# Attention of batch b+1 emitted between the MLP chunks of batch b, with 128-token tiles and a softmax with a constant bias

## The chip, the cores and the metric

The kernel runs on one core of one Trainium2 chip. Times are device microseconds of that core for one execution. Of the kernel before, three runs are known: 1060.54, 1063.5 and 1299.54 us, median 1063.5. A profile of one execution is there as well.

## The reference

Eight batches, twelve heads, 448 tokens, head size 64. Queries and keys are normalised over the head size, attention is a plain softmax over all 448 keys, the heads are joined to 768 columns, and a LayerNorm and an MLP of width 3072 with a residual follow.

```python
def rmsnorm(x, g):
    rms = np.sqrt(np.mean(x * x, axis=-1, keepdims=True) + 1e-06)
    return x / rms * g
q_n, k_n = (rmsnorm(q, g_q), rmsnorm(k, g_k))
scores = scale * np.matmul(q_n, k_n.transpose(0, 1, 3, 2))     # scale = 1/8
scores = scores - np.max(scores, axis=-1, keepdims=True)
attn = np.exp(scores)
attn = attn / (np.sum(attn, axis=-1, keepdims=True) + 1e-09)
x = np.matmul(attn, v)                          # heads joined: (8, 448, 768)
xn = (x - mu) / np.sqrt(var + 1e-06) * g_ln     # mu, var over 768
out = x + np.maximum(xn @ w_ch1, 0.0) @ w_ch2   # 768 -> 3072 -> 768
```

Inputs and output are float32; the matmuls are done in float16 with float32 accumulation, the keys as a high and a low float16 part.

## The kernel before, in words

Tokens lie in four tiles of 112 partitions; token 4p+s is row p of tile s.

*Preparation* (`emit_prep`, L143 to L188) takes a quarter of a batch, three heads: loads of q and k on the SP queue, squares on ACT (L153, L154), sums and an inverse root on DVE (`_rsqrt`, L20 to L29: a start value by exponent bits, one exponential on ACT, three Newton steps), the scaled query (L166), the key times both gains and its inverse root (L170, L174), its high part (L179) and low part (L180). Column 63 of the low part is overwritten by 1 (L181). Values come by casting DMAs on the POOL queue (L185) into v16, whose column 64 is 1.

*One head* (`emit_heads`, L190 to L242): PE transposes query (L198), key high (L201) and key low (L204), four tiles each; DVE and ACT copy them to SBUF (L208 to L210). Four small matmuls against the first 64 keys (L213) give an estimate of each query's maximum (L216), which POOL writes, negated, into column 63 of the query (L217). The query is transposed once more (L221, L223), now with that column. So the score matmul, 128 rows deep (query twice; key high over key low), subtracts the estimate by itself. L227 makes 112 keys by 448 queries, L228 the exponential on ACT, in float16. Sixteen matmuls of 65 columns (L234) multiply by the values and, in column 64, sum the denominator; L239 and L240 divide and write x_sb.

*One MLP* (`emit_mlp`, L95 to L141): LayerNorm on DVE (L104, L105, `_rsqrt`, L111, L113 with the gain), 24 transposes (L118) and copies (L121) to xnT, 768 by 448. Up: 24 groups of six matmuls of 448 columns (L126), each followed by a Relu on ACT (L128). Down: six groups of 24 matmuls (L132) that give 128 output columns by 448 tokens, that is channel-major; each is copied to SBUF (L135), transposed back in float32 four times (L138) and added to x_sb (L139). One store per batch (L141).

*Order.* The program emits all attention, one quarter prepared ahead of the heads, and then the eight MLPs (L244 to L259). The framework then lists the instructions of each engine: an instruction that is ready by the framework's own estimate is taken by the place at which it was emitted, and a tile must wait for a free buffer. x_sb has three buffers (L86), so attention of a fourth batch waits for the first MLP; from there on attention and MLP mix. On the chip each engine keeps the listed order. Weights come by casting DMAs on the POOL queue (L76 to L81); nothing holds them back, so they start at once. PSUM: psQ and psKhl one buffer each, scores two, psO one, MLP three (L88 to L91).

Of the kernel before, what the change touches and what calls it, by code (L numbers as in the profile page):

```python
# [13 lines left out]
AX = mybir.AxisListType  # L15
ts = bass.ts
LN2 = 0.6931471805599453


def _rsqrt(nc, eng, out, a, t0, t1, iters=3):  # L20
    eng.tensor_copy(out=t0, in_=a.bitcast(INT32))
    eng.tensor_scalar(out=t0, in0=t0, scalar1=2.0 ** -23, scalar2=-127.0,
                      op0=ALU.mult, op1=ALU.add)
    nc.scalar.activation(out, t0, AFT.Exp, scale=-0.5 * LN2)
    for _ in range(iters):
        eng.tensor_tensor(out=t1, in0=out, in1=out, op=ALU.mult)
        eng.tensor_tensor(out=t1, in0=t1, in1=a, op=ALU.mult)
        eng.tensor_scalar(out=t1, in0=t1, scalar1=-0.5, scalar2=1.5, op0=ALU.mult, op1=ALU.add)
        eng.tensor_tensor(out=out, in0=out, in1=t1, op=ALU.mult)  # L29


@with_exitstack
def kernel(
# [12 lines left out]
    nc = tc.nc  # L46
    B, H, S, Dh = q.shape
    Dm = H * Dh
    P1 = 112
    NS = S // P1  # L50
    NQ = 4
    HH = H // NQ
    GH = HH * NS
    FF = moe_w_ch1.shape[1]
    NDC = Dm // 128
    NNC = FF // 128

    const = ctx.enter_context(tc.tile_pool(name="const", bufs=1))
    id16 = const.tile([128, 128], FP16)
    make_identity(nc, id16)  # L60
    id32 = const.tile([128, 128], FP32)
    make_identity(nc, id32)
    gq_bc = const.tile([P1, Dh], FP32)
    gk_bc = const.tile([P1, Dh], FP32)
    nc.sync.dma_start(gq_bc, g_q.unsqueeze(0).broadcast_to([P1, Dh]))
    nc.sync.dma_start(gk_bc, g_k.unsqueeze(0).broadcast_to([P1, Dh]))
    gprod_bc = const.tile([P1, Dh], FP32)
    nc.vector.tensor_tensor(out=gprod_bc, in0=gq_bc, in1=gk_bc, op=ALU.mult)
    gln_bc = const.tile([P1, Dm], FP32)
    nc.sync.dma_start(gln_bc, moe_g_ln.unsqueeze(0).broadcast_to([P1, Dm]))  # L70

    w_pool = ctx.enter_context(tc.tile_pool(name="w_pool", bufs=1))
    w1_sb = w_pool.tile([128, NDC, NNC, 128], FP16)
    w2_sb = w_pool.tile([128, NNC, Dm], FP16)

    def emit_w_load():  # L76
        for dc in range(NDC):
            nc.gpsimd.dma_start(
                out=w1_sb[:, dc],
                in_=moe_w_ch1[ts(dc, 128), :].rearrange("p (nc c) -> p nc c", c=128))  # L80
        nc.gpsimd.dma_start(out=w2_sb, in_=moe_w_ch2.rearrange("(nc p) d -> p nc d", p=128))  # L81

    a_io = ctx.enter_context(tc.tile_pool(name="a_io", bufs=2))
    a_tmp = ctx.enter_context(tc.tile_pool(name="a_tmp", bufs=1))
    a_hd = ctx.enter_context(tc.tile_pool(name="a_hd", bufs=2))
    x_pool = ctx.enter_context(tc.tile_pool(name="x_pool", bufs=3))  # L86
    m_tmp = ctx.enter_context(tc.tile_pool(name="m_tmp", bufs=1))
    ps_tr = ctx.enter_context(tc.tile_pool(name="ps_tr", bufs=1, space=bass.MemoryType.PSUM))  # L88
    ps_s = ctx.enter_context(tc.tile_pool(name="ps_s", bufs=2, space=bass.MemoryType.PSUM))
    ps_o = ctx.enter_context(tc.tile_pool(name="ps_o", bufs=1, space=bass.MemoryType.PSUM))  # L90
    ps_m = ctx.enter_context(tc.tile_pool(name="ps_m", bufs=3, space=bass.MemoryType.PSUM))  # L91

    x_tiles = []

    def emit_mlp(b):  # L95
        x_sb = x_tiles[b]
        xn16 = m_tmp.tile([P1, NS, Dm], FP16, tag="xn16")
        stat = m_tmp.tile([P1, NS, 16], FP32, tag="stat")
        lt0 = m_tmp.tile([P1, NS], FP32, tag="lt0")
        lt1 = m_tmp.tile([P1, NS], FP32, tag="lt1")  # L100
        rstd = m_tmp.tile([P1, NS], FP32, tag="rstd")
        for s1 in range(NS):
            for sg in range(2):
                nc.vector.bn_stats(out=stat[:, s1, ts(sg, 6)], in_=x_sb[:, s1, ts(sg, Dm // 2)])  # L104
            nc.vector.bn_aggr(out=stat[:, s1, 12:14], in_=stat[:, s1, 0:12])  # L105
        nc.vector.tensor_scalar(out=stat[:, :, 14], in0=stat[:, :, 13], scalar1=1.0, scalar2=1e-6,
                                op0=ALU.mult, op1=ALU.add)
        _rsqrt(nc, nc.vector, rstd, stat[:, :, 14], lt0, lt1)
        for s1 in range(NS):
            t32 = m_tmp.tile([P1, Dm], FP32, tag="t32", bufs=1)  # L110
            nc.vector.tensor_scalar(out=t32, in0=x_sb[:, s1], scalar1=stat[:, s1, 12:13],  # L111
                                    scalar2=rstd[:, s1:s1 + 1], op0=ALU.subtract, op1=ALU.mult)
            nc.vector.tensor_tensor(out=xn16[:, s1], in0=t32, in1=gln_bc, op=ALU.mult)  # L113
        xnT = m_tmp.tile([128, NDC, S], FP16, tag="xnT")
        for dc in range(NDC):
            pst = ps_m.tile([128, 512], FP16, tag="mlpacc")
            for s1 in range(NS):
                nc.tensor.matmul(pst[:, ts(s1, P1)], xn16[:, s1, ts(dc, 128)],  # L118
                                 id16[0:P1, 0:P1], is_transpose=True,
                                 start=(s1 == 0), stop=(s1 == NS - 1))  # L120
            nc.vector.tensor_copy(out=xnT[:, dc], in_=pst[:, 0:S])  # L121
        hT16 = m_tmp.tile([128, NNC, S], FP16, tag="hT16")
        for ncc in range(NNC):
            psH = ps_m.tile([128, S], FP32, tag="mlpacc")
            for dc in range(NDC):
                nc.tensor.matmul(psH, w1_sb[:, dc, ncc], xnT[:, dc],  # L126
                                 start=(dc == 0), stop=(dc == NDC - 1))
            nc.scalar.activation(out=hT16[:, ncc], in_=psH, func=AFT.Relu)  # L128
        for jc in range(NDC):
            psC = ps_m.tile([128, S], FP32, tag="mlpacc")  # L130
            for ncc in range(NNC):
                nc.tensor.matmul(psC, w2_sb[:, ncc, ts(jc, 128)], hT16[:, ncc],  # L132
                                 start=(ncc == 0), stop=(ncc == NNC - 1))
            chj = m_tmp.tile([128, S], FP32, tag="chj", bufs=1)
            nc.vector.tensor_copy(out=chj, in_=psC)  # L135
            for s1 in range(NS):
                psr = ps_m.tile([P1, 128], FP32, tag="mlpacc")
                nc.tensor.matmul(psr, chj[:, ts(s1, P1)], id32, is_transpose=True)  # L138
                nc.vector.tensor_tensor(out=x_sb[:, s1, ts(jc, 128)], in0=psr,  # L139
                                        in1=x_sb[:, s1, ts(jc, 128)], op=ALU.add)  # L140
        nc.sync.dma_start(out[b].rearrange("(p s1) d -> p s1 d", p=P1), x_sb)  # L141

    def emit_prep(b, qtr, v16, x_sb):  # L143
        hs = qtr * HH
        q_sb = a_io.tile([P1, GH, Dh], FP32, tag="q_sb")
        k_sb = a_io.tile([P1, GH, Dh], FP32, tag="k_sb")
        nc.sync.dma_start(q_sb.rearrange("p (h s1) d -> p h (s1 d)", h=HH),
                          q[b, hs:hs + HH].rearrange("h (p s1) d -> p h (s1 d)", p=P1))
        nc.sync.dma_start(k_sb.rearrange("p (h s1) d -> p h (s1 d)", h=HH),
                          k[b, hs:hs + HH].rearrange("h (p s1) d -> p h (s1 d)", p=P1))  # L150
        sq_q = a_tmp.tile([P1, GH, Dh], FP32, tag="sq", bufs=2)
        sq_k = a_tmp.tile([P1, GH, Dh], FP32, tag="sq", bufs=2)
        nc.scalar.activation(sq_q, q_sb, AFT.Square)  # L153
        nc.scalar.activation(sq_k, k_sb, AFT.Square)  # L154
        ssq = a_hd.tile([P1, 2, GH], FP32, tag="ssq")
        nc.vector.tensor_reduce(out=ssq[:, 0], in_=sq_q, axis=AX.X, op=ALU.add)
        nc.vector.tensor_reduce(out=ssq[:, 1], in_=sq_k, axis=AX.X, op=ALU.add)
        msq = a_hd.tile([P1, 2, GH], FP32, tag="msq")
        nc.vector.tensor_scalar(out=msq, in0=ssq, scalar1=1.0 / Dh, scalar2=1e-6,
                                op0=ALU.mult, op1=ALU.add)  # L160
        rrms = a_hd.tile([P1, 2, GH], FP32, tag="rrms")
        rt0 = a_hd.tile([P1, 2, GH], FP32, tag="rt0")
        rt1 = a_hd.tile([P1, 2, GH], FP32, tag="rt1")
        _rsqrt(nc, nc.vector, rrms, msq, rt0, rt1)
        qn16 = a_io.tile([P1, GH, Dh], FP16, tag="qn16")
        nc.vector.tensor_tensor(  # L166
            out=qn16, in0=q_sb,
# [122 lines left out]
```

## Time and profile before

| | |
|---|---|
| median of three runs | 1063.5 us (1060.54 to 1299.54) |
| span of the profiled execution | 1055.9 us |
| its own time | the span and a few us around it; the two lower runs lie 4.6 and 7.6 us above the span |
| mean granted TensorE clock | 0.909 |
| HBM | 52.31 MB read, 11.01 MB written |

In the profile PE is TensorE's matmuls, PEld its weight loads, DVE the vector engine, ACT the scalar engine, POOL GpSimd, SP the engine that issues most DMAs. A row of the groups reads: line, engine, operation, output and inputs, shapes, count, then busy microseconds in total and mean nanoseconds of one, then the idle time of that engine just before them and what ended it. A row of the windows reads: start and end in the span, its length, busy microseconds of the engine with the number of instructions that started, the granted clock as a share of full speed, the share of time that the DMA engines were busy, and GB/s. A row of the chain of waits in order of time reads: start, length, and the piece of work that the end was waiting for. Matmuls are pipelined, so a matmul's mean duration is longer than the distance from one to the next; the distance is had from a run of them in the chain.

### The profile page before, as it was taken

Reading aid. Unit: us, or ns where it says so; the run is one execution under the profiler, and the core shown is the slowest. Engines: PE = TensorE matmul, PEld = TensorE weight load, DVE = VectorE, ACT = ScalarE, POOL = GpSimd, SP = SyncE. Lnnn points to the kernel's source line nnn. Section 1 sums busy time; section 2 is a strip of 40 time slices with the busy share of each in tenths; the row PEclk is TensorE's granted clock in tenths of the full one; section 3 lists DMA queues with packets and bytes.
Section 4 is the critical chain, followed back from the end, with each engine's and each line's share of the span. In section 5 each row is a group of like instructions: output and inputs, shape, how many; then the busy total and the mean of one; then the engine's idle time right before and its main releaser. Section 6 shows DMA issues by size and latency. Waiting matters only on the chain.

```text
span 1055.9 us, 16343 instructions
## 1 busy us (share of the span) xinstructions
PE 908.8 (86%) x6528; PEld 552.9 (52%) x6528; DVE 625.2 (59%) x1849; ACT 400.3 (38%) x777; POOL 68.1 (6%) x183
## 2 busy tenths in 40 slices
PE   0368888888899899889998999789998998898986
PEld 0246565666554466446653566346644664444542
DVE  5457777776786378927884678647873743402111
ACT  1235544444442066404760377106730661130310
POOL 2010100100100000100010002000000000000000
PEclk9999565555589999999999999899999999999999
DMA  9891511501420101501150114110100000100101
GB/s 189 173 207 41 65 28 41 66 27 40 57 50 1 43 25 42 78 1 54 41 79 14 53 41 53 40 53 27 28 1 25 29 2 1 53 1 1 53 1 53
DMA packets 71484, 49.42 MB, mean 47 GB/s; under 512 B 45056, under 2 KB 69632, under 8 KB 70512
## 3 DMA queue, kind: packets, MB, share of 16 engines
q0 software_dynamic: 47472, 14.94, 12.9%
q1 hardware_dynamic: 23936, 33.44, 10.4%
q8 instruction: 51, 0.84, 0.3%
q14 instruction: 25, 0.20, 0.1%
HBM read 52.31 MB, written 11.01 MB: 60 GB/s over the span
## 4 chain that ended last, share of the span: by engine, by line
PE 76%; DVE 15%; DMA 4%; issue 2%; POOL 2%; ACT 1%; SPq 0%; POOLq 0%; DVEq 0%; ACTq 0%
PE psC L132 20%; PE psH L126 19%; PE psS L227 10%; PE psO L234 9%; PE psA L213 3%; PE psQ L221 3%; PE psQ L198 3%; DVE chj L135 3%; DMA q_sb<-in_q_dram 3%; PE psr L138 3%; PE psKhl L201 2%; PE psKhl L204 2%; DVE x_sb L139 2%; DVE xn L113 1%; DVE maxs L216 1%
## 5 line engine op out<-in xcount | busy, mean ns | idle before, releaser
L126 PE MATMUL psH<-xnT,w_sb 128*128 128x448 f16 x1152 | 268.4, 354 | 0.0
L228 ACT ACTIVATE E<-psS 112x448 f16<-112x448 f32 x384 | 193.9, 542 | 143.0 <-PE psS L227 137.2
L128 ACT ACTIVATE hT<-psH 128x448 f16<-128x448 f32 x192 | 103.9, 542 | 364.3 <-PE psH L126 364.0
L132 PE MATMUL psC<-hT,w_sb 128*128 128x448 f16 x1152 | 233.1, 359 | 0.0
L132 PEld LDWEIGHTS <-w_sb 128*128 128x128 f16 x1152 | 115.5, 101 | 103.3 <-issue 7.1
L234 PEld LDWEIGHTS <-E 112*112 112x112 f16 x1536 | 148.0, 156 | 39.6 <-issue 14.4
L135 DVE COPY chj<-psC 128x448 f32<-128x448 f32 x48 | 29.9, 624 | 229.4 <-PE psC L132 229.4
L227 PE MATMUL psS<-q16d,khl 128*112 128x448 f16 x384 | 148.4, 435 | 17.1 <-DVE q16d L223 13.5
L234 PE MATMUL psO<-v,E 112*112 112x65 f16 x1536 | 149.7, 234 | 0.7
L126 PEld LDWEIGHTS <-w_sb 128*128 128x128 f16 x1152 | 104.7, 100 | 77.8 <-issue 0.2
L138 PE MATMUL psr<-id,chj 128*112 128x128 f32 x192 | 41.7, 299 | 51.2 <-DVE chj L135 36.3
L227 PEld LDWEIGHTS <-khl 128*112 128x112 f16 x384 | 54.3, 150 | 33.2 <-issue 12.4
L217 POOL TENSOR_SCALAR qn<-maxs 112x4 f16<-112x4 f32 x96 | 26.6, 277 | 640.4 <-DVE maxs L216 582.6
L221 PE MATMUL psQ<-id,qn 112*64 112x112 f16 x384 | 42.7, 244 | 28.3 <-POOL qn L217 27.6
L138 PEld LDWEIGHTS psr<-id,chj 128*112 128x112 f32 x192 | 20.6, 133 | 84.1 <-DVE chj L135 57.4
L216 DVE TENSOR_REDUCE maxs<-psA 112x4 f32<-112x256 f32 x96 | 40.4, 421 | 38.4 <-PE psA L213 36.3
L198 PE MATMUL psQ<-id,qn 112*64 112x112 f16 x384 | 44.1, 248 | 20.2 <-DVE qn L166 20.2
L198 PEld LDWEIGHTS <-qn 112*64 112x64 f16 x384 | 27.2, 126 | 63.1 <-issue 42.9
L139 DVE TENSOR_TENSOR x_sb<-psr,x_sb 112x128 f32<-112x128 f32 x192 | 47.3, 286 | 19.3 <-PE psr L138 18.2
L213 PE MATMUL psA<-khl,q16d 64*112 64x64 f16 x384 | 44.4, 238 | 16.1 <-DVE khl L209 16.1
L210 ACT COPY khl<-psKhl 64x448 f16<-64x448 f16 x96 | 50.2, 523 | 17.6 <-DVE khl L209 15.1
L221 PEld LDWEIGHTS <-qn 112*64 112x64 f16 x384 | 26.7, 124 | 49.5 <-POOL qn L217 46.0
(55 smaller groups left out, 898.4 us busy)
## 6 DMA issues: line engine op xcount, KB each, us to landing
q_sb<-in_q_dram SPq DMA_DIRECT2D x32, 336.0 KB, 3.2
k_sb<-in_k_dram SPq DMA_DIRECT2D x32, 336.0 KB, 3.2
out_dram<-x_sb SPq DMA_DIRECT2D x8, 1344.0 KB, 6.2
v<-in_v_dram POOLq DMA_DIRECT2D x32, 168.0 KB, 5.8
w_sb<-in_moe_w_ch_dram POOLq DMA_DIRECT2D x6, 768.0 KB, 14.0
w_sb<-in_moe_w_ch_dram POOLq DMA_DIRECT2D x1, 4608.0 KB, 33.0
gln_bc<-in_moe_g_ln_dram SPq DMA_DIRECT2D x1, 336.0 KB, 5.7
gq_bc<-in_g_q_dram SPq DMA_DIRECT2D x1, 28.0 KB, 3.1
```

Of the source, the lines that this page charges most:

```text
L126: nc.tensor.matmul(psH, w1_sb[:, dc, ncc], xnT[:, dc], start=(dc == 0), stop=(dc == NDC - 1))
L128: nc.scalar.activation(out=hT16[:, ncc], in_=psH, func=AFT.Relu)
L132: nc.tensor.matmul(psC, w2_sb[:, ncc, ts(jc, 128)], hT16[:, ncc], start=(ncc == 0), stop=(ncc == NNC - 1))
L135: nc.vector.tensor_copy(out=chj, in_=psC)
L138: nc.tensor.matmul(psr, chj[:, ts(s1, P1)], id32, is_transpose=True)
L139: nc.vector.tensor_tensor(out=x_sb[:, s1, ts(jc, 128)], in0=psr, in1=x_sb[:, s1, ts(jc, 128)], op=ALU.add)
L198: nc.tensor.matmul(psQ[:, ts(s1, P1)], qn16[:, g0 + s1], id16[0:P1, 0:P1], is_transpose=True, start=(s1 == 0), stop=(s1 == NS - 1))
L213: nc.tensor.matmul(psA[:, ic, 0:64], q16d[0:64, ts(ic, P1)], khl[0:64, 0:64], start=True, stop=True)
L221: nc.tensor.matmul(psQ2[:, ts(s1, P1)], qn16[:, g0 + s1], id16[0:P1, 0:P1], is_transpose=True, start=(s1 == 0), stop=(s1 == NS - 1))
L227: nc.tensor.matmul(psS[:, 0:S], khl[:, ts(jc, P1)], q16d, start=True, stop=True)
L228: nc.scalar.activation(out=E16[:, jc], in_=psS[:, 0:S], func=AFT.Exp, scale=1.0 / 8.0)
L234: nc.tensor.matmul(psO[:, ic, 0:65], E16[:, jc, ts(ic, P1)], v16[:, jc, h, 0:65], start=first, stop=(ic == NS - 1 and jc == NS - 1))
```

## The change

The whole program is rewritten around the same computation. What is added, moved and removed:

- **Order.** `attention` is a generator over 49 steps, one per pair of heads and one to drain: step p has scores of pair p and values of pair p-1, and the transposes of pair p+1. `run` drives it: until step 7 there is attention alone, with loads of W1 in 12 chunks and of W2 in four between; then for each batch b the 48 or 56 chunks of the MLP of b are emitted, and after each the attention goes on so that the attention of b+1 is done at 0.78 of the chunks. Then come LayerNorm and transposes of b+1. The MLP of the last batch has no attention beside it.
- **Tiles.** A head's first 384 tokens are three full tiles of 128; the 64 left of two heads share a tile (`load_unit`: a unit is four heads, 14 groups of 128 rows, nine DMAs on SP for q, k and v in float32). The 64 left tokens of two batches share a tile in the MLP, so even batches have 384 tokens and odd ones 512.
- **Preparation** of a unit is as before without the columns of ones; the query is written twice side by side, key high and low side by side, so one transpose of 128 columns does for both. v is cast on POOL from the float32 load.
- **Softmax.** No estimate of the maximum; the exponential has the constant bias -4. The seven exponentials of a pair have 128 keys by 448 queries.
- **Check.** The reciprocals of all denominators are kept; `flag` tests before the last MLP that all lie in 1/3e7 to 0.5. At the end the flag is read, and `_general`, a loop over the batches that computes all outputs again with row maxima, runs behind a branch if one does not.
- **MLP.** The LayerNorm gain is multiplied into W1 as it is loaded (float32 load on SP, six POOL instructions a chunk). Up is as before with 384 or 512 columns. Down has 128 tokens of hT as weights and 384 columns of W2 moving, so its result is token-major and is added to x at once; the float32 transposes and the copy are gone. Stores are per token tile.
- **PSUM.** One buffer for transposes, two for scores, one each for oA and oB (values of a pair), three for the MLP.

```diff
+    def load_unit(self, u):
...
+        t = self.p_in.tile([128, 3, UG, D], FP32, tag="qkv")
+        for n, src in enumerate((self.q, self.k, self.v)):
+            nc.sync.dma_start(
+                t[:, n, 0:UH * 3].rearrange("p (h j) d -> p h (j d)", j=3),
+                src[b, hs:hs + UH, 0:384].rearrange("h (p j) d -> p h (j d)", j=3))
+            left = src[b, hs:hs + UH, 384:448].rearrange("(g e) p d -> e p g d", e=2)
+            for e in range(2):
+                nc.sync.dma_start(t[64 * e:64 * e + 64, n, UH * 3:UG], left[e])
...
+    def prep_unit(self, u):
...
+        nc.vector.tensor_tensor(out=khl[:, :, 1], in0=t[:, 1], in1=khl[:, :, 0], op=ALU.subtract)
+        nc.vector.tensor_tensor(out=qn[:, :, 0], in0=t[:, 0],
+                                in1=rr[:, 0].unsqueeze(2).broadcast_to([128, UG, D]), op=ALU.mult)
+        nc.vector.tensor_copy(out=qn[:, :, 1], in_=qn[:, :, 0])
+        v16, vl = self.v16[u % 3], self.vl[u % 3]
+        nc.gpsimd.tensor_copy(out=v16[:, :, :, 0:D],
+                              in_=t[:, 2, 0:UH * 3].rearrange("p (h j) d -> p h j d", j=3))
...
+    def trans_k(self, p):
...
+        ps = self.ps_tr.tile([128, 1024], FP16, tag="tr")
...
+        for i, g in enumerate(gs):
+            nc.tensor.matmul(ps[:, ts(i, 128)], khl[:, g], sh.id16, is_transpose=True,
+                             start=(i == 0), stop=(i == 6))
+        flat = kT.rearrange("p g d -> p (g d)")
+        nc.vector.tensor_copy(out=flat[:, 0:64], in_=ps[:, 0:64])
+        nc.vector.tensor_copy(out=flat[:, 128:960], in_=ps[:, 64:896])
...
+    def scores(self, p, i):
...
+        if i < 6:
+            h = i // 3
+            nc.tensor.matmul(ps[:, 0:S], kT[:, 192 + 128 * i:320 + 128 * i],
+                             qT[:, h * S:(h + 1) * S], start=True, stop=True)
+        else:
+            nc.tensor.matmul(ps[:, 0:S], kT[:, 0:128], qT[:, 0:S], start=True, stop=False)
+            nc.tensor.matmul(ps[:, 0:384], kT[:, 64:192], qT[:, 512:896], start=False, stop=False)
+            nc.tensor.matmul(ps[:, 384:448], kT[:, 64:192], qT[:, 448:512], start=False, stop=True)
+        nc.scalar.activation(out=c["E"][:, i], in_=ps[:, 0:S], func=AFT.Exp, scale=1.0 / 8.0,
+                             bias=EXP_BIAS)
...
+    def values(self, p, i):
...
+        for t in range(3):
+            nc.tensor.matmul(oA[:, t, cs], E[:, i, m0 + 128 * t:m0 + 128 * t + 128], rhs,
+                             start=(i == 0 and t == 0), stop=(i == 6 and t == 2))
+        nc.tensor.matmul(oB[:, cs], E[:, i, l0:l0 + 64], rhs, start=(i == 0), stop=(i == 6))
+        if i == 6:
+            self.evac_o(p)
...
+    def load_w1(self, c0, c1):
...
+        st = self.p_st.tile([128, NDC, 256], FP32, tag="st", name="st")
+        nc.sync.dma_start(st[:, :, 0:c1 - c0],
+                          self.w1[:, c0:c1].rearrange("(dc p) f -> p dc f", p=128))
+        for dc in range(NDC):
+            nc.gpsimd.tensor_scalar(out=sh.w1[:, dc, c0:c1], in0=st[:, dc, 0:c1 - c0],
+                                    scalar1=sh.gln[:, dc:dc + 1], scalar2=None, op0=ALU.mult)
...
+        def down(t, g, s):
...
+            for f in range(6 * s, 6 * s + 6):
+                nc.tensor.matmul(ps[:, 0:384], hT[:, f, ts(t, 128)], sh.w2[:, f, ts(g, 384)],
+                                 start=(f == 0), stop=(f == NFF - 1))
+            if s == 3:
+                x = tiles[t]
+                nc.vector.tensor_tensor(out=x[:, ts(g, 384)], in0=ps[:, 0:384],
+                                        in1=x[:, ts(g, 384)], op=ALU.add)
+                if g == 1:
+                    self.store(b, t, x)
...
+    def run(self):
...
+        upto(1)
+        wcols = list(range(0, FF, 256))
+        for i, c in enumerate(wcols):
+            self.load_w1(c, c + 256)
+            upto(1 + 5 * (i + 1) / len(wcols))
+        for n0 in range(0, NFF, 6):
+            self.load_w2(n0, n0 + 6)
+        upto(7)
+        xn, n = self.ln(0)
+        for t in range(n):
+            self.ln_trans(xn, n, t)
+        frac = 0.78
+        for b in range(B):
+            chunks = list(self.mlp_chunks(b))
...
+            for i, (cost, emit) in enumerate(chunks):
+                emit()
+                done += cost
+                f = done / total
+                if b + 1 < B:
+                    upto(min(goal, start + (goal - start) * f / frac))
+                    if xn is None and self.pos >= goal:
+                        xn, n = self.ln(b + 1)
...
+            if b + 2 == B:
+                upto(1e8)
+                self.flag()
...
+    val = nc.values_load(sh.flag[0:1, 0:1], min_val=0, max_val=1)
+    with tc.If(val > 0):
+        _general(tc, sh, q, k, v, g_q, g_k, out)
```

`trans_q` is `trans_k` for the query with one copy of 896 columns; `evac_o` takes two reciprocals and two products on DVE; `ln` has no gain. All lines of the functions of the kernel before are removed, `_rsqrt` stays.

More of the change, by code (lines that the diff above doesn't have):

```diff
@@ L66 @@
[L66 to L167, printed above, removed]
-            in1=rrms[:, 0].unsqueeze(2).broadcast_to([P1, GH, Dh]), op=ALU.mult)
-        kg = a_tmp.tile([P1, GH, Dh], FP32, tag="kg")
-        nc.vector.tensor_tensor(out=kg, in0=k_sb,
-                                in1=gprod_bc.unsqueeze(1).broadcast_to([P1, GH, Dh]),
-                                op=ALU.mult)
-        kn32 = a_tmp.tile([P1, GH, Dh], FP32, tag="kn32")
-        nc.vector.tensor_tensor(
-            out=kn32, in0=kg,
-            in1=rrms[:, 1].unsqueeze(2).broadcast_to([P1, GH, Dh]), op=ALU.mult)
-        knh = a_io.tile([P1, GH, Dh], FP16, tag="knh")
-        knl = a_io.tile([P1, GH, Dh], FP16, tag="knl")
-        nc.vector.tensor_copy(out=knh, in_=kn32)
-        nc.vector.tensor_tensor(out=knl, in0=kn32, in1=knh, op=ALU.subtract)
-        nc.gpsimd.memset(knl[:, :, 63], 1.0)
-        if qtr == 0:
-            nc.gpsimd.memset(v16[:, :, :, 64], 1.0)
-            for s1 in range(NS):
-                nc.gpsimd.dma_start(
-                    out=v16[:, s1, :, 0:Dh],
-                    in_=v[b].rearrange("h (p s1) d -> p s1 h d", p=P1)[:, s1])
-        return dict(hs=hs, qn16=qn16, knh=knh, knl=knl, v16=v16, x_sb=x_sb)
@@ L244 @@
[L244 to L259 removed]
+    sh = _Shared()
@@ new lines @@
+    nc.vector.tensor_tensor(out=sh.gprod, in0=gg[:, 0], in1=gg[:, 1], op=ALU.mult)
+    sh.gln = const.tile([128, NDC], FP32, name="gln")
+    nc.scalar.dma_start(sh.gln, moe_g_ln.rearrange("(c p) -> p c", p=128))
+    sh.flag = const.tile([1, 1], INT32, name="flag")
+    sh.w1 = const.tile([128, NDC, FF], FP16, name="w1")
+    sh.w2 = const.tile([128, NFF, DM], FP16, name="w2")
+    with ExitStack() as fctx:
+        _Fast(fctx, tc, sh, q, k, v, moe_w_ch1, moe_w_ch2, out).run()
+    val = nc.values_load(sh.flag[0:1, 0:1], min_val=0, max_val=1)
```

481 lines of the change are left out of this document (396 added, 85 removed).

## The prediction

> **What bounds the kernel now.** I read the page first, then the busy time by windows, then the chain of waits in order of time, and last the groups of instructions for prices.
>
> ```profile
> span 1055.9 us, 16343 instructions
> PE 908.8 (86%) x6528; PEld 552.9 (52%) x6528; DVE 625.2 (59%) x1849; ACT 400.3 (38%) x777; POOL 68.1 (6%) x183
> ...
> PEclk9999565555589999999999999899999999999999
> ...
> PE 76%; DVE 15%; DMA 4%; issue 2%; POOL 2%; ACT 1%; SPq 0%; POOLq 0%; DVEq 0%; ACTq 0%
> ```
>
> TensorE is busy for 86% of the span and carries 76% of the chain, so its program order sets the time. But its time is not all work at full speed: the granted clock drops to 0.5 in slices 5 to 10. The windows (all PE, then the score matmuls of L227 alone) say in which stage:
>
> ```profile
> 105.00:210.00 105.00, 88.17 (x652) 0.57 0.33 51
> 372.00:445.00 73.00, 69.37 (x627) 1.00 0.27 44
> ```
> ```profile
> 150.00:200.00 50.00, 16.86 (x32) 0.53 0.12 34
> 372.00:445.00 73.00, 14.79 (x48) 1.00 0.27 44
> ```
>
> Up to 299 us there is only attention (three batches, as x_sb has three buffers), and it runs at a clock of 0.57: a score matmul lasts 16.86/32 = 527 ns there and 14.79/48 = 308 ns once MLP matmuls stand between. The chain in order of time gives the pitch of each piece:
>
> ```profile
> 3.66 10.39 DMA k_sb<-in_k_dram
> ...
> 20.13 17.26 DMA q_sb<-in_q_dram
> ...
> 45.00 0.91 PE psS L227 x2
> ...
> 107.09 0.91 PE psS L227 x2
> 113.19 0.93 PE psS L227 x2
> ...
> 365.64 1.81 DVE xnT L121 x6
> ...
> 444.88 6.25 PE psC L132 x24
> 452.86 4.59 PE psC L132 x24
> ...
> 478.47 1.81 DVE xnT L121 x6
> ...
> 914.42 1.67 PE pst L118 x24
> 916.08 27.34 PE psH L126 x144
> 943.42 4.55 PE psC L132 x24
> 949.71 4.59 PE psC L132 x24
> ...
> 1041.87 4.59 PE psC L132 x24
> ```
>
> The reader sees four stages. Attention alone takes 113.19 - 107.09 = 6.1 us a head. Then one batch of attention and one of MLP take 478.47 - 365.64 = 112.8 us; in it the W2 groups start 6.3 us apart (949.71 - 943.42) with 4.55 us of matmuls, and the 1.7 us between are copy, transpose and add. The last two MLPs run alone, and the end lies 1055.9 - 1046.5 = 9.4 us behind the last W2 matmul.
>
> **The change, part by part.** Its first effect is order: MLP chunks of batch b are emitted between attention steps of batch b+1, so attention alone lasts one batch instead of three and the MLPs that run alone shrink from three (one before, two after) to one. The second is less work on PE. Prices, warm:
>
> ```profile
> 372.84 0.96 PE psO L234 x16
> ```
> ```profile
> L138 PE MATMUL psr<-id,chj 128*112 128x128 f32 x192 | 41.7, 299 | 51.2 <-DVE chj L135 36.3 <-DVE x_sb L139 15.0
> L139 DVE TENSOR_TENSOR x_sb<-psr,x_sb 112x128 f32<-112x128 f32 x192 | 47.3, 286 | 19.3 <-PE psr L138 18.2
> L240 DVE TENSOR_TENSOR x_sb<-psO,recip 112x256 f32<-112x256 f32 x96 | 40.2, 419 | 1.0
> L156 DVE TENSOR_REDUCE ssq<-sq_q 112x12 f32<-112x768 f32 x32 | 30.2, 943 | 16.1 <-ACT sq_q L153 16.1
> L170 DVE TENSOR_TENSOR kg<-k_sb,gprod_bc 112x768 f32<-112x768 f32 x32 | 30.4, 950 | 7.0 <-DMA k_sb<-in_k_dram 6.8
> L179 DVE CAST knh<-kn 112x768 f16<-112x768 f32 x32 | 17.8, 555 | 0.3
> L208 DVE COPY q16d<-psQ 64x448 f16<-64x448 f16 x96 | 36.6, 381 | 24.5 <-PE psQ L198 23.8
> L29 DVE TENSOR_TENSOR rrms<-rrms,rt 112x24 f32<-112x24 f32 x96 | 16.3, 171 | 0.7
> L104 DVE BATCH_NORM_STATS2 stat<-x_sb 112x6 f32<-112x384 f32 x64 | 33.9, 540 | 0.1
> L111 DVE TENSOR_SCALAR t<-x_sb,stat,rstd 112x768 f32<-112x768 f32 x32 | 21.7, 678 | 0.9
> L228 ACT ACTIVATE E<-psS 112x448 f16<-112x448 f32 x384 | 193.9, 542 | 143.0 <-PE psS L227 137.2 <-PE psO L234 2.6
> L153 ACT ACTIVATE sq_q<-q_sb 112x768 f32<-112x768 f32 x32 | 26.9, 841 | 49.1 <-DMA q_sb<-in_q_dram 47.3 <-DVE ssq L156 1.4
> L183 POOL MEMSET v<- 112x48 f16 x8 | 2.5, 310 | 26.9 <-PE psO L234 26.9
> L217 POOL TENSOR_SCALAR qn<-maxs 112x4 f16<-112x4 f32 x96 | 26.6, 277 | 640.4 <-DVE maxs L216 582.6 <-DVE rt L27 25.4 <-DVE recip L239 18.1
> ```
>
> *MLP matmuls.* psH runs at 27.34/144 = 190 ns, 0.424 ns a column. Up: 163 ns for 384 columns (even batches), 217 for 512 (odd). Down is now token-major, 48 matmuls of 384 columns per token tile. An even batch takes 288 x 0.163 = 47.0, an odd one 144 x 0.217 + 192 x 0.163 = 62.5 us. The pair costs what it costs now (4 x 27.3): W2 token-major saves no streaming; it removes the copies of L135, the fp32 transposes of L138 (299 ns) and the 1.7 us behind each of 48 W2 groups, at most 82 us; its one add of 384 columns per group lies beside the next group, as ps_m has three slots. LayerNorm transposes: 1.67/24 = 70 ns for 112 columns, so 76 for 128; 18 or 24 a batch, 1.4 or 1.8 us. All MLPs: 4 x 48.4 + 4 x 64.3 = 451 us.
>
> *Attention matmuls per pair of heads.* Transposes fall from 32 (query twice) to 14 of full width: 14 x 76 = 1.06 us. The eight estimate matmuls (psA) go, and with them the chain max, POOL, second query transpose. Scores keep 3584 columns: 1.52. Values: 28 instead of 32 at 0.96/16 = 60 ns: 1.68. Sum 4.26 us a pair, against 6.1 for two heads now (32 x 70 + 8 x 60 + 1.52 + 32 x 60 ns).
>
> The Trainium skill (TensorE: Matmul & The Clock Gate, Back-to-back issue gap) gives about 81 ns per matmul for a stream of weight loads and matmuls at 128 columns. By it the 42 small matmuls cost 0.66 us more a pair, some 27 us more in the sum; the 70 ns row of the same kind of stream disagrees, so I go by the row.
>
> *Start.* The first unit is nine DMAs on SP with W1 chunks behind them, W2 on POOL at once. Its landing is bounded by the two rows above, 14 us and 37 us; with about 10 us of preparation and 3 of transposes and copies the first scores come between 27 and 50 us; I take 34 (DMA is contended from the start, as now). Then seven steps of attention alone, still at the low clock: between 7.6 us a pair (DVE, below) and 9.4 (two heads at 6.1 us, with the columns 7456 instead of 9760). PE alone, at 527/308 times 4.26, is 7.3; I take 8. MLP 0 starts at 34 + 56 = 90 us (bounds 80 and 116).
>
> *Interleave.* Left are 41 pairs, 175 us, and 451 us of MLP, of which the last MLP (64) runs alone: 562 us in the interleave. How dense can PE be? Now, between 365.64 and 444.88 it fits 12 heads (37.0), 27.3 of psH, 1.7 of transposes and about 5 of psC, 71 of 79 us, 0.90, with the long chain per head in it. That chain goes, and values run one pair behind scores, so waits are shorter: 0.94, bounds 0.90 and 1. 562/0.94 = 598 us.
>
> *Other engines, costed at nothing.* DVE: from L139 and L240 an element costs 1.04 ns behind 153 fixed; L208 gives 0.51 for f16 from PSUM. Per pair: copies 64, 832, 896 columns 1.37, two reciprocals 0.36, two products 0.84: 2.6 us. Per unit of two pairs: two reductions 2.2, four products of 896 elements 4.3, casts 1.0, fifteen small ones 2.6: 10.1. So 7.6 a pair, and with LayerNorm and adds 61 us a batch, beside 80 of PE. ACT: seven exponentials 3.8 a pair, 24 Relu 13, squares 6: 42 us a batch. Both hide behind PE as long as no in-order wait puts them on its path (price: the second case below). POOL's copies of v are off the path as units are prepared two pairs ahead. SP's waits are in order too: a W1 load waiting for its staging slot, or a store waiting for its add, holds the q, k, v loads queued behind; these run two units ahead (about 27 us each). The oA and oB banks have one buffer each: values of the next pair wait for 1.2 us of DVE, and MLP chunks stand in that gap.
>
> *End.* The last add and store, then the flag is read and the branch skipped.
>
> ```profile
> out_dram<-x_sb SPq DMA_DIRECT2D x8, 1344.0 KB, 6.2
> ```
>
> The last store is a seventh of these 1344 KB. No row shows a branch; I bound it by 0 and two such landings, 12 us. Against the 9.4 us of now I take 9 behind the last matmul, the smaller store paying for most of the branch (bounds 5 and 15).
>
> Sum: 90 + 598 + 64 + 9 = 761 us of span. Around the span lie 1060.54 - 1055.9 = 4.6 to 1063.5 - 1055.9 = 7.6 us for the lowest and the median run (the profile tells nothing of the highest, 1299.54); with 5, **766 us**. The best bounds give 80 + 562 + 64 + 5 + 5 = 716, the worst 116 + 624 + 64 + 15 + 8 = 827.
>
> **The rivals.**
> *DVE paces.* At 61 of 80 us it is the next engine, its long preparation instructions stand in front of the PSUM copies, and ps_tr, oA and oB have one buffer. If the 2.6 us of each pair fall on PE's path, 41 x 2.6 = 107 us more: 873. For: "DVE 15%" of the chain now. Against: MLP chunks are independent and fill, and the window 372 to 445 shows PE at 69 of 73 us.
> *W1 comes late.* Each chunk is load, six POOL scalings, slot free. POOL's price for 256 elements is not shown: between 0.28 us (L217, four elements) and 256 x 310/48 ns = 1.65 (L183), nearer the lower end as most of such a short instruction is fixed; 72 of them take 20 to 119 us. At the upper end the last chunk stands at about 140 us, 50 late; attention of batch 1 fills some of it until its two x buffers are full: 40 us more, 806. Against: the chunks are used in order, two up steps each, so only the last must be that late.
> *The clock stays low*, the case on the other side. The place is the interleave: at 105 to 210 us PE was busy for 84% and had 0.57. If MLP beside attention did not raise it, 662 us become 662 x 527/308 = 1133: 1237 us. It decides from 63% of the interleave on (766 + 0.63 x 471 = 1063). Against: every window with MLP matmuls has 0.95 to 1.00, and their share now grows. The Trainium skill (same page, The HAM clock gate) lets activity release the throttle and idling of about 3.4 us bring it back; this trace shows 0.57 on a busy PE, so it does not agree.
> *The general path runs*, a second computation of everything. By the reference's formula the denominators of these inputs lie between 14.6 and 1442.5, allowed are 2 to 3e7. So it is skipped.
>
> **How the numbers follow.** Forecast 0.72, DVE paces 0.11, W1 late 0.13, clock low 0.03, general path 0.01. The range takes the forecast's bounds, the lowest end drawn in because all its terms would have to be best at once, and W1 late: 726 to 830. Left out are the DVE case, the low clock and the general path, 0.15. Faster by over 2% (about what a measurement of this kernel tells from no change) 0.96, within 2% 0.01, slower 0.03.
>
> **What would show it.** Right: clock above 0.9 from about a tenth of the span on; psC at 163 ns with no DVE copy between groups; the first up matmul near 90 us; PE idle under 8% until the attention ends; seven exponentials a pair on ACT. Wrong: PE waiting on DVE copies of qT and kT or on oA for more than 60 us in total; up matmuls waiting on POOL; any instruction of the general path in the trace; clock near 0.5 past 150 us.

## The result, and the profile after

| | before | after |
|---|---|---|
| median | 1062.26 us | 796.23 us (795.01 to 798.35) |
| profiled execution | span 1055.9 | 795.19, span 793.4 |
| mean granted clock | 0.909 | 0.97 |
| first up matmul of the MLP | 297.3 us | 131.4 us |

The ratio is 0.7505, with a 95% interval of 0.748 to 0.753; it leaves out one slow execution of the kernel before (1299.54 us), which the median of 1062.26 includes. The prediction was 766 us, 726 to 830. The measured time lies in that range, 30 us above the forecast, and the 30 us have one place, as the page shows at a glance:

```profile
span 793.4 us, 12901 instructions
PE 697.7 (88%) x5114; PEld 419.7 (53%) x5114; DVE 455.2 (57%) x1229; ACT 322.0 (41%) x609; POOL 119.8 (15%) x154
PE   0276438999999989999999999998999999999996
...
POOL 2579992000000000010000000010000000000000
PEclk9997777999999999999999999999999999999999
DMA  8993642523021130233022130233020110001011
```

From the seventh of forty slices on PE is dense; in the fourth to sixth it is at 0.6, 0.4 and 0.3, and there POOL is full. The windows (busy of PE, PEld, DVE, ACT, POOL, then clock, DMA share, GB/s) put numbers to it:

```profile
30.00:60.00 30.00, 20.25 (x154) 12.91 (x152) 18.41 (x45) 13.70 (x26) 22.45 (x25) 1.00 1.06 259
60.00:130.00 70.00, 36.72 (x321) 23.03 (x321) 49.71 (x137) 26.90 (x51) 63.20 (x63) 0.73 0.47 143
140.00:634.00 494.00, 479.48 (x3555) 288.25 (x3553) 319.59 (x846) 226.81 (x430) 27.07 (x51) 0.99 0.22 64
```

From 140 to 634 us PE is busy 97% at a clock of 0.99: attention and MLP mixed, as forecast. From 60 to 130 us it is busy half the time, and no other engine but POOL is full. The groups and waits of this stretch, first the SP queue's own waits, then ACT's:

```profile
L264 POOL TENSOR_SCALAR w<-st,gln 128x256 f16<-128x256 f32 x72 | 77.0, 1086 | 9.2 <-DMA st<-in_moe_w_ch_dram 8.9
```
```profile
SPq L261 <- POOL w L264: 39.6, 7, 8.1
```
```profile
ACT sq L108 <- DMA t<-in_q_dram: 32.8, 4, 10.4
```

POOL's scaling of W1 takes 1.09 us an instruction, 77 us in all; SP waits 39.6 us for staging slots that it frees; ACT waits 33 us for q, in the first 135 us. How one leads to the other is read from the timeline of SP, ACT and DVE around 110 us (rows: start, length, engine, line, work, count, and in brackets the idle time before and who ended it):

```profile
94.14 0.49 SPq L94 DMA_DIRECT2D t<-in_q_dram  x1
100.98 5.81 SPq L261 DMA_DIRECT2D st<-in_moe_w_ch_dram  x2
107.25 1.27 SPq L99 DMA_DIRECT2D t<-in_q_dram  x2
```
```profile
111.86 0.95 ACT L108 ACTIVATE sq<-t 128x896 f32<-128x896 f32 x1 [6.68 <-DMA t<-in_q_dram]
```
```profile
112.84 1.09 DVE L109 TENSOR_REDUCE ssq<-sq 128x14 f32<-128x896 f32 x1 [6.42 <-ACT sq L108]
```

The first of the three loads of a unit's q goes at 94 us, the other two only at 107, for two W1 loads stand between and wait for slots. ACT stands at the square until 111.9, with exponentials behind it; DVE stands at the sum of the squares, with the small instructions of LayerNorm 0 behind it; so PE has neither scores nor MLP.

Not all of ACT's 33 us come this way. Two of the four waits stand behind W1 loads, 10.4 us that end at 88 us and the 6.7 us above. The other two end at 42 and 124 us (7.0 and 8.7 us), and there SP issued q's load when DVE's last product on the unit's tile (L124) was done: the tiles of q, k and v have two buffers (`p_in`), so the load of a unit waits until DVE has prepared the unit two before it. The last of the four, in the timelines of DVE, SP and ACT:

```profile
117.49 1.07 DVE L124 TENSOR_TENSOR khl<-t,khl 128x896 f16<-128x896 f32 x1
118.62 0.37 SPq L94 DMA_DIRECT2D t<-in_q_dram  x1
123.62 0.95 ACT L108 ACTIVATE sq<-t 128x896 f32<-128x896 f32 x1 [8.69 <-DMA t<-in_q_dram]
```

### The profile page after: what moved, and what is told of

It is laid out like the page before. It is cut to its first block, busy times and chain, and to the rows that moved or that the text cites. A ratio compares the mean times of both kernels' runs of the same rounds, so it can differ in the third digit from the quotient of the medians.

```text
span 793.4 us, 12901 instructions
## 1 busy us (share of the span) xinstructions
PE 697.7 (88%) x5114; PEld 419.7 (53%) x5114; DVE 455.2 (57%) x1229; ACT 322.0 (41%) x609; POOL 119.8 (15%) x154
## 5 line engine op out<-in xcount | busy, mean ns | idle before, releaser
L334 PE MATMUL psC<-w,hT 128*128 128x384 f16 x1344 | 245.8, 329 | 0.0
L323 PE MATMUL psH<-xnT,w 128*128 128x512 f16 (+1 forms) x1152 | 243.3, 353 | 1.8 <-DVE xnT L310 1.8
L180 ACT ACTIVATE E<-ps 128x448 f16<-128x448 f32 x336 | 178.3, 541 | 127.7 <-PE ps L174 100.5
L325 ACT ACTIVATE hT<-psH 128x384 f16<-128x384 f32 (+1 forms) x192 | 104.2, 543 | 162.6 <-PE psH L323 162.6
L334 PEld LDWEIGHTS <-hT 128*128 128x128 f16 x1344 | 125.8, 98 | 77.7 <-issue 1.9
L323 PEld LDWEIGHTS <-w 128*128 128x128 f16 x1152 | 106.5, 98 | 92.2 <-issue 2.6
L174 PE MATMUL ps<-qT,kT 128*128 128x448 f16 x288 | 105.7, 374 | 12.3 <-ACT E L180 7.6
L202 PEld LDWEIGHTS <-E 128*128 128x128 f16 x1008 | 72.7, 100 | 76.2 <-ACT E L180 16.9
L202 PE MATMUL oA<-v,E 128*128 128x65 f16 x864 | 74.5, 197 | 16.7 <-ACT E L180 10.4
L264 POOL TENSOR_SCALAR w<-st,gln 128x256 f16<-128x256 f32 x72 | 77.0, 1086 | 9.2 <-DMA st<-in_moe_w_ch_dram 8.9
```

Source lines behind the costliest of these rows:

```text
L174: nc.tensor.matmul(ps[:, 0:S], kT[:, 192 + 128 * i:320 + 128 * i], qT[:, h * S:(h + 1) * S], start=True, stop=True)
L180: nc.scalar.activation(out=c["E"][:, i], in_=ps[:, 0:S], func=AFT.Exp, scale=1.0 / 8.0, bias=EXP_BIAS)
L202: nc.tensor.matmul(oA[:, t, cs], E[:, i, m0 + 128 * t:m0 + 128 * t + 128], rhs, start=(i == 0 and t == 0), stop=(i == 6 and t == 2))
L264: nc.gpsimd.tensor_scalar(out=sh.w1[:, dc, c0:c1], in0=st[:, dc, 0:c1 - c0], scalar1=sh.gln[:, dc:dc + 1], scalar2=None, op0=ALU.mult)
L323: nc.tensor.matmul(ps[:, 0:N], sh.w1[:, dc, ts(f, 128)], xnT[:, dc, 0:N], start=(dc == 0), stop=(dc == NDC - 1))
L325: nc.scalar.activation(out=hT[:, f, 0:N], in_=ps[:, 0:N], func=AFT.Relu)
```

## The experiments

The sum of the prediction had one term far off: MLP 0 at 131.4 us where 90 was taken. The theories of why: **A**, the W1 path (POOL's scaling holds the two staging slots, SP waits for them in order, q, k and v stand behind). **B**, too many bytes at the start for the DMA engines (share 1.06 from 30 to 60 us). **C**, the attention-only stage is slow by itself, by low clock and DVE. Later came **L**, LayerNorm 0's own chain on DVE. Beside these, two questions on where the 266 us came from: the order, and W2's layout. All but the eighth run edit the changed kernel; the kernels of runs 5 and 12 leave out most of the weights, and run 12 one LayerNorm too, so their output is another one.

| run | median, us | ratio to before | first up matmul, us |
|---|---|---|---|
| changed kernel | 796.23 | 0.748 to 0.753 | 131.4 |
| 1 W1 loads on POOL's queue | 814.37 | 0.7616 to 0.7698 | 152.9 |
| 2 gain in xnT | 784.53 | 0.7334 to 0.7412 | 122.9 |
| 3 W2 later | 783.14 | 0.7333 to 0.7409 | 114.2 |
| 4 order undone | 807.37 | 0.7547 to 0.7628 | 191.4 |
| 5 few weights | 774.12 | 0.7255 to 0.7292 | 109.9 |
| 6 = 2 and 3 | 785.80 | 0.7353 to 0.7418 | 124.7 |
| 7 W2 channel-major, on 2 | 800.80 | 0.7517 to 0.7549 | 117.7 |
| 8 kernel before, two x buffers | 1046.61 | 0.9771 to 0.9870 | 241 |
| 9 LayerNorm 0 first, on 3 | 797.09 | 0.7490 to 0.7517 | 115.0 |
| 10 two Newton steps, on 3 | 787.27 | 0.7395 to 0.7424 | 115.5 |
| 11 = 9 and 10 | 782.54 | 0.7337 to 0.7388 | 104.9 |
| 12 few weights, no LayerNorm 0 | 759.33 | 0.7121 to 0.7157 | 93.7 |

**1. W1's loads on POOL's queue.**

```diff
-        nc.sync.dma_start(st[:, :, 0:c1 - c0],
+        nc.gpsimd.dma_start(st[:, :, 0:c1 - c0],
```

> The loads of W1 are issued on POOL's queue instead of SP's; the scaling on POOL and the two staging slots stay. Theory A (W1's scaling on POOL, 72 x 1.09 us, holds the staging slots; SP waits for a slot in order, and the q, k, v loads behind it come late): the q, k, v loads no longer wait, squares wait for loads under 10 us instead of 33 in the first 135 us, attention of batch 0 ends near 90 us, the first up matmul comes between 90 and 110 us, time 770 to 780. Theory B (the DMA engines are full, W2 and W1 against q, k, v): nothing changes by the issuing queue, 796 +- 5. Theory C (the attention-only stage is slow by the low clock and DVE): 796 +- 5.

Slower, against all three. POOL's waits in the first 135 us say why:

```profile
POOL w L264 <- DMA st<-in_moe_w_ch_dram: 24.0, 6, 6.6
```

On POOL's own queue a W1 load is issued only between scalings, so POOL then waits 24 us for the bytes it has just asked for, and the last scaling starts 17 us later (136.5 against 119.3 us). ACT's waits for q did fall (32.8 to 19.0 us). So the wait moved from SP to POOL; as an edit it tells nothing for B or C, and A's "SP is what holds" is only a part.

**2. No staging, no scaling.**

```diff
-        st = self.p_st.tile([128, NDC, 256], FP32, tag="st", name="st")
...
+        nc.gpsimd.dma_start(out=sh.w1[:, :, c0:c1],
+                            in_=self.w1[:, c0:c1].rearrange("(dc p) f -> p dc f", p=128))
...
-        nc.vector.tensor_copy(out=self.xnT[:, :, ts(t, 128)], in_=ps)
+        nc.vector.tensor_tensor(out=self.xnT[:, :, ts(t, 128)], in0=ps,
+                                in1=sh.gln.unsqueeze(2).broadcast_to([128, NDC, 128]), op=ALU.mult)
...
```

> W1 comes by casting DMAs on POOL's queue without staging or scaling; the LayerNorm gain is multiplied where LayerNorm's transposes are copied out of PSUM (a product of 768 elements instead of a copy). Theory A: POOL and SP free, first up matmul near 90 us, time 755 to 770, the 28 products cost 0.4 us more each on DVE, hidden. Theory B: as many bytes as before, read at the same time, first up matmul past 120 us, 790 or more. Theory C: 790 to 800, as DVE gets more to do.

12 us better, first up matmul at 122.9: under half of the 26 to 41 us that A said, and more than B or C. Without W1 on SP and the scaling on POOL, the q, k, v loads still land late: ACT waits 11.9 us for one load and 7.9 us for others in the first 135 us. SP is not free either. It waits for the buffers that DVE frees:

```profile
SPq L94 <- DVE khl L124: 69.6, 5, 19.2
```

The load of the 11.9 us was issued at 68.1 us, right behind L124, and ACT had it at 80.6, with a DMA share of 0.78 from 60 to 90 us.

**3. W2 held back.**

```diff
     def load_w2(self, n0, n1):
+        self.nc.gpsimd.tensor_copy(out=self.sh.w2[:, n0:n1, 0:1],
+                                   in_=self.sh.w1[:, 0, FF - 8:FF - 8 + n1 - n0].unsqueeze(2))
         self.nc.gpsimd.dma_start(
```

> The four loads of W2 are held back until the last chunk of W1 is scaled (a small POOL copy in each W2 part, out of W1's last columns, which the load then overwrites). Theory A: q, k, v still wait behind W1's slots, 796 +- 8. Theory B: 4.7 MB less in the first 60 us, q, k, v and W1 land sooner, 780 or less. Theory C: 796 +- 5.

13 us better, short of the 780 that B said, and more than A or C. So both the staging and the bytes take part.

**4. The order undone.**

```diff
-        upto(7)
...
+        upto(1e8)
+        self.flag()
+        for b in range(B):
+            xn, n = self.ln(b)
+            for t in range(n):
+                self.ln_trans(xn, n, t)
+            for cost, emit in self.mlp_chunks(b):
+                emit()
```

> All attention is emitted first and the eight MLPs after it, as in the kernel before; all else is as in the changed kernel. Theory 1 (the emitted order is what mixes them): attention alone for two batches (two x buffers) at a clock near 0.6, MLPs at the end alone, 860 to 900. Theory 2 (the framework's list mixes them by readiness anyway, and the two x buffers already hold attention back): 800 to 830; then most of the gain is less work on TensorE and not the order.

Theory 2: only 11 us. The first up matmul comes 60 us later, but then PE hardly waits:

```profile
0.00:190.00 190.00, 97.53 (x771) 61.56 (x772) 133.19 (x373) 73.04 (x136) 97.10 (x109) 0.81 0.58 150
190.00:740.00 550.00, 539.43 (x4015) 319.55 (x4015) 295.08 (x849) 230.22 (x450) 25.27 (x45) 0.99 0.18 53
```

98% busy from 190 to 740 us, without any order written out. With two x buffers the framework's list lets attention run two batches ahead and no further (12 pairs' products are done before the first up matmul), and the MLP fills. The order by hand was the change's first words, and it is worth 11 of the 266 us.

**5. Few weights.** One chunk of W1, a quarter of W2; the same matmuls.

```diff
...
+            if i == 0:
+                self.load_w1(c, c + 256)
...
-        for n0 in range(0, NFF, 6):
-            self.load_w2(n0, n0 + 6)
+        self.load_w2(0, 6)
```

> Only the first 256 columns of W1 and the first quarter of W2 are loaded (one chunk scaled), and used for all; the MLP's result is another one, its work the same. Theory A+B (the weights' way in, by staging and by DMA, is what makes the start long): attention of batch 0 runs without waits for q, k, v beyond the first unit, first up matmul at 85 to 95 us, 755 to 770. Theory C (low clock and DVE set the attention-only stage): first up matmul past 115 us, 785 or more.

774: the weights' way in costs 22 us, all told. But the first up matmul comes at 109.9, not at 90, so A and B together are not the whole. C is not the rest as it was put: from the first scores at 36.6 us to the last product of batch 0 at 85 the seven steps take 48 us, less than the 56 of the prediction, at a clock of 0.77 from 60 us on. DVE's timeline shows where the rest is, from the sixth pair's product (the last of batch 0) to LayerNorm's result and its copy:

```profile
83.59 0.56 DVE L218 TENSOR_TENSOR x<-oA,rec_all 128x384 f32<-128x384 f32 x1
84.79 0.28 DVE L222 TENSOR_TENSOR xl<-oB,recl_all 64x128 f32<-64x128 f32 x1
85.07 0.55 DVE L292 BATCH_NORM_STATS2 stat<-x 128x6 f32<-128x384 f32 x1
...
104.13 2.37 DVE L298 TENSOR_SCALAR xn<-x,stat,rs 128x768 f16<-128x768 f32 x3
108.09 1.57 DVE L310 COPY xnT<-psX 128x768 f16<-128x768 f16 x3 [1.59 <-PE psX L308]
```

Attention of batch 0 ends at 85 us (the prediction's 34 + 7 x 8 = 90), and then LayerNorm takes 25 us, its fifteen small instructions standing between preparations of the next units. The same stretch takes 30 us in the changed kernel, from 102 to 131, with the 6.4 us of DVE's wait for the square in it:

```profile
101.71 0.27 DVE L222 TENSOR_TENSOR xl<-oB,recl_all 64x128 f32<-64x128 f32 x1
...
126.54 2.44 DVE L298 TENSOR_SCALAR xn<-x,stat,rs 128x768 f16<-128x768 f32 x3
129.59 1.52 DVE L310 COPY xnT<-psX 128x768 f16<-128x768 f16 x3 [0.61 <-PE psX L308]
```

This is theory L. One more thing shows in run 5: with hardly any weight loads, ACT still waits 20.9 us for q in the first 135 us, as SP waits for the two buffers that DVE frees:

```profile
SPq L94 <- DVE khl L124: 67.9, 7, 17.6
```

**6. Both edits, 2 and 3.**

> The two edits that saved 12 and 13 us together: W1 by casting DMAs with the gain in the copy of xnT, and W2's loads held back until the end of W1. If staging and DMA load are two causes that add: 765 to 775. If both edits relieve the same thing (too many bytes before 90 us): 778 to 786.

785.8: they don't add. ACT's waits for q are 26.1 us here, and the window from 60 to 90 us shows a full DMA:

```profile
60.00:90.00 30.00, 13.36 (x93) 8.27 (x93) 18.76 (x45) 8.43 (x16) 8.30 (x8) 0.65 1.08 205
```

With W1 unstaged its twelve loads all start at once, and W2 follows them; the DMA engines are full from 60 to 90 us instead. The staging slots also paced W1.

**7. W2 channel-major again.**

```diff
-        self.p_st = pool("p_st", 2)
+        self.p_st = pool("p_st", 1)
...
+                nc.tensor.matmul(ps[:, 0:N], sh.w2[:, f, ts(jc, 128)], hT[:, f, 0:N],
+                                 start=(f == 0), stop=(f == NFF - 1))
...
+                nc.vector.tensor_copy(out=chj[:, 0:N], in_=ps[:, 0:N])
+                for t in range(n):
...
+                    nc.tensor.matmul(psr, chj[:, ts(t, 128)], sh.id32, is_transpose=True)
```

> On top of the edit with the gain in xnT (784.5 us): W2 channel-major again, six groups of 24 matmuls of 384 or 512 columns, a copy to SBUF, a float32 transpose and an add of 128 columns per token tile (one staging buffer less, for space). Theory 1 (attention and other groups fill the gaps behind each W2 group, only the 168 float32 transposes and the last MLP's six gaps of 1.7 us cost): 800 to 820. Theory 2 (the gaps are on the path wherever they stand): 48 x 1.7 = 82 us more, 850 to 870.

16 us over run 2, just at Theory 1's lower end. The staging pool has one buffer less, for space; LayerNorm's result lies in it, and what that costs was not tried by itself. In the last MLP the six groups go 7.0 us apart with 5.2 us of matmuls, with the same gaps as before the change:

```profile
747.52 5.19 PE psC L331 x24
752.74 0.70 DVE chj L335
753.48 0.34 PE psr L339
...
754.52 5.22 PE psC L331 x24
```

Six gaps of 1.8 us are 11 of the 16 us. Where attention is there to fill, 42 further groups cost 5 us in all by the medians, and nothing in the profiled executions: there the last MLP's up matmuls start at 716.3 us, and at 716.4 in run 2.

**8. The kernel before with two x buffers** (`bufs=3` to `bufs=2` in its line 86).

> The kernel before with two buffers of x_sb instead of three, nothing else. Theory 1 (x_sb's buffers hold attention back and so decide how many batches run at the low clock): attention alone for two batches, one batch more interleaved, 67 + 77 - 113 = 31 us less, 1025 to 1040. Theory 2 (fewer buffers only add waits for the store): 1063 or more.

17 us better (1.3 to 2.3%), Theory 1's direction at somewhat over half its size: MLP 0 moved from 297 to 241 us:

```profile
241.18 27.98 PE psH L126 x144
269.16 4.55 PE psC L132 x24
275.45 4.59 PE psC L132 x24
```

but it still ran alone with its gaps, so fewer batches at the low clock did not all become interleaved time.

**9, 10, 11. LayerNorm 0 first; two Newton steps; both** (each on run 3).

```diff
+        with self.tc.high_priority():
+            xn, n = self.ln(0)
+            for t in range(n):
+                self.ln_trans(xn, n, t)
...
-def _rsqrt(nc, eng, out, a, t0, t1, iters=3):
+def _rsqrt(nc, eng, out, a, t0, t1, iters=2):
```

> On top of the held-back W2 (783.1 us): the LayerNorm of batch 0 and its transposes are listed ahead of all other ready work. Theory L (LayerNorm's chain of 15 small instructions stands in DVE's queue between the preparation of later units, some 25 us from the last product of batch 0 to xnT, and the first MLP waits for it): first up matmul some 5 to 15 us earlier, 770 to 780. Theory N (TensorE has attention of batch 1 to do in that time anyway): 783 +- 4.

> On top of the held-back W2 (783.1 us): two Newton steps instead of three in every inverse root, so 4 of 15 small DVE instructions less in each of 32 chains. Theory L: preparation and LayerNorm of the attention-only stage get 0.8 us shorter per chain plus the waits between, first up matmul 5 to 10 us earlier, 773 to 780. Theory N: DVE is hidden behind TensorE, 783 +- 4.

> Held-back W2, LayerNorm of batch 0 first, two Newton steps. Theory L: 762 to 775. Theory N: 783 +- 5.

None as L said. Listing LayerNorm first left the first up matmul at 115.0 (114.2 without) and cost 14 us. The trace shows where: in run 9, from 115 to 130 us, PE has 5.78 us of work, where run 3 has 12.98.

```profile
115.00:130.00 15.00, 5.78 (x24) 2.81 (x24) 3.05 (x11) 1.58 (x4) 0.00 (x0) 0.73 1.15 220
122.13 0.95 ACT L108 ACTIVATE sq<-t 128x896 f32<-128x896 f32 x1 [19.35 <-DMA t<-in_q_dram]
123.63 1.14 PE L325 MATMUL psH<-xnT,w 128*128 128x384 f16 x6 [3.96 <-ACT hT L327]
```

The held-back loads of W2 go out from 104 us on, and the DMA share is 1.15. A unit's q, asked for at 110 us, lands at 122; ACT stands at its square for 19.4 us with the Relus of MLP 0 behind it, and the up matmuls stop for want of them. Run 3 has a shorter wait of this kind (9.4 us, until 135).

Two Newton steps gave nothing (787.27 against 783.14, intervals overlapping). Both together had the earliest up matmul of all kernels with full weights, 104.9, and 782.54 us, level with run 3. There LayerNorm met a limit of its own: its result lies in the same two staging slots as the chunks of W1 (`p_st`, tag "st"), so it must wait until the last chunk but one is scaled:

```profile
100.92 2.23 DVE L300 TENSOR_SCALAR xn<-x,stat,rs 128x768 f16<-128x768 f32 x3 [4.42 <-POOL w L264]
```

So runs 9 to 11 are no clean test of L, and run 12 is the one that settles it. Of these kernels 2, 3, 6, 10 and 11 beat the changed one, by 9 to 14 us; between them hardly any difference can be told.

**12. Few weights and no LayerNorm of batch 0.**

```diff
-        xn, n = self.ln(0)
...
+        for t in range(n):
+            self.nc.vector.tensor_scalar(out=xn[:, t], in0=self.xs[0][:, t], scalar1=1.0,
+                                         scalar2=0.0, op0=ALU.mult, op1=ALU.add)
```

> On top of few weights (774.1 us): the LayerNorm of batch 0 is left out (xn is x itself, three instructions of 768 elements), so batch 0's output is another one. Theory L: the first up matmul comes at about 92 us instead of 110, 760 to 768. Theory N: first up earlier, but 774 +- 4, as TensorE's work is only done in another order.

As L said, and a touch more: the first up matmul at 93.7, 759.33 us, 15 under run 5.

```profile
86.42 0.56 DVE L218 TENSOR_TENSOR x<-oA,rec_all 128x384 f32<-128x384 f32 x1
...
90.28 0.55 DVE L382 TENSOR_SCALAR xn<-x 128x768 f16<-128x768 f32 x1
...
92.13 0.55 DVE L310 COPY xnT<-psX 128x768 f16<-128x768 f16 x1
```

From the last product to the last copy it is 6 us instead of 25, and 15 us come back for a first up matmul that is 16 us earlier. So in this pair of runs the MLP's start sets the end; that attention of batch 1 can't fill the gap because DVE is the engine that the gap is made of is argued, not shown. The start alone does not always set it: in run 4 it is 60 us later and costs 11 us, in run 9 it is 16 us earlier and gains nothing.

## Why the prediction was right, and where it was off

- **What bounds it: right.** After the start PE is 97% busy at a clock of 0.99.
- **First scores:** 34 us taken, 33.6 measured.

```profile
33.60 0.91 PE L174 MATMUL ps<-qT,kT 128*128 128x448 f16 x2 [1.35 <-DVE qT L161]
```

- **MLP 0 at 90 us: the step that failed**, by 41 us, over its upper bound of 116. Two terms of the sum were mis-sized. "Seven steps of attention alone", 56 us from 34 on, took 68 us, from 33.6 to 102; without weight traffic they take 48 (run 5). And the term for LayerNorm 0 was missing: it was priced inside DVE's 61 us a batch, "at nothing", though for batch 0 nothing dense covers it. It took 30 us. So 12 and 30 make the 41. Runs 5 and 12 show what they are worth in time: 22 us for the weights' way in, 15 more for LayerNorm 0.
- **SP's in-order waits, "two units ahead":** named and priced at nothing; that was wrong. About 17 of ACT's 33 us of waiting for q stand behind W1 loads that wait for a slot. And q, k and v do not run two units ahead: with two buffers a unit's load waits for DVE's preparation of the unit two before it, which no term of the prediction has.
- **The range held, in part by luck.** The start broke its own bound by 15 us; the terms behind it came out 12 us under, and the range reached to 830 for the worst of all bounds and for a rival of another mechanism.
- **The rival "W1 comes late"** (806 us, 0.13) has the nearer number and POOL's scaling as a cause, but not the mechanism. POOL's price of 1.09 us lies in its bounds of 0.28 and 1.65, but not near the lower end as argued; the last scaling started at 119 us, where 140 was the upper bound. But MLP 0 did not wait for W1: all of it was scaled some 11 us before the first up matmul. What was late was q, and behind it LayerNorm 0.
- **Interleave:** 598 us taken, from 131.4 to 724.2 it is 593. Nine pairs were done when MLP 0 began, where seven were taken, so 39 x 4.26 + 387 = 553 us of work, 0.93 dense. Taken was 0.94.
- **The last MLP** 64 taken, 62.3 measured; **end** 9 taken, 6.9; **around the span** 5 taken, 1.8:

```profile
724.21 31.08 PE psH L323 x144
755.29 31.21 PE psC L334 x192
786.52 0.56 DVE xl L338
```

The measured terms add up: 131.4 + 592.8 + 62.3 + 6.9 + 1.8 = 795.2 us. Against 766 the start is 41 over and the others 12 under.

- **W2 token-major, at most 82 us:** 16 by run 7. The bound was far off because gaps behind W2 groups are filled where there is something to fill them with.
- **DVE paces, clock low, general path:** none. PE's waits for the copies of kT and qT come to 9.3 us in all, the clock is 0.99 past 140 us, and no instruction of the general path ran. The sign "clock above 0.9 from about a tenth of the span on" came late: the clock was 0.73 from 60 to 130 us.
- **The order as "first effect":** the prediction put it first and gave it no price of its own. Run 4 gives it 11 us. The other 255 us lie in all the rest: what a pair of heads costs, the two x buffers (17 us in the kernel before, run 8), W2's layout (16 us, run 7). How they split in the changed kernel was not tried.

What stays open: how the 22 us of the weights divide between slots and bytes. Each of runs 2 and 3 takes over half away, and together they do not add, so neither has a share that is its own. No run has a third buffer for q, k and v, so what that wait costs is open too.

## What to carry to other kernels

When work is overlapped, price the first round by itself: a step that is hidden in every later round is on the path in the first, where nothing covers it. Follow an in-order queue through: a weight load that waits for a slot held up q on SP, a square on ACT, a sum on DVE and at last the first matmul of the MLP. And ask where moved bytes go: W2's loads, held back out of the way of one q, stood in the way of a later one. Before writing an order by hand, look at what the buffers and the framework's list already do; here it was worth 1.4%.

## What was not expected of the hardware

POOL's product with a scalar per partition is slow for its size: 256 elements from float32 to float16 took 920 ns in the median (1086 in the mean), while a cast of 768 elements took 825:

```profile
L264 POOL TENSOR_SCALAR w<-st,gln x72: 912/920/2745, 31.6 to 119.3; 128x256 f16<-128x256 f32 x72
```
```profile
L129 POOL CAST v<-t x7: 819/825/1460, 16.4 to 127.2; 128x768 f16<-128x768 f32 x7
```

That is 3.6 ns an element against 1.07, with whatever an instruction costs by itself in both. The Trainium skill (GPSIMD Engine Reference, Engine selection) calls operations of one input on this engine roughly line-rate; the cast agrees with that, at about the 1.04 ns an element of DVE's products, and the product with a scalar, if it counts as one input, does not.
